# A scheduled SSM convolution and feed-forward kernel: GpSimd's powers planned around VectorE's port, idle matmuls on zeros ahead of the taps, and a full-height skip row

## The chip, the cores and the metric

The kernel runs on one core of a Trainium2 chip. The time is the device time of that core in microseconds (us), the median of several executions. A ratio is the mean time of one kernel's runs over the mean time of the other kernel's runs of the same rounds, on the same chip; it is therefore not quite the ratio of the medians that are quoted beside it. The brackets after a ratio are its 95% interval. A profile shows a single execution, and single executions of one kernel differ here by about 1 us, at times more. So a profile is used to find where the time lies. Eviction means the copy of a result out of PSUM, the memory that PE writes to; X0 is the dense transform of the first block of VectorE's products.

## The reference, cut to what matters

```python
# q, k, v: 1 x 2048 x 640;  shift_k: 640 x 4;  ssm_k: 640 x 2048;  ssm_D: 640
k_shift = sum(k_pad[:, t:t+S, :] * shift_k[:, 3-t] for t in range(4))   # four taps
kv = k_shift * v
y  = irfft(rfft(kv_pad) * rfft(ssm_k_pad))[:S] + kv * ssm_D             # long convolution, skip row
a  = q * y
# ... residual and layer norm (two layers), then the feed-forward part:
out = (silu(h @ w_gate) * (h @ w_up)) @ w_down                          # 640 x 1728
```

The convolution is done as dense transforms on TensorE (PE) with products of spectra on VectorE (DVE). The rows are handled in four blocks.

## The kernel before

The program does not list its instructions in the order in which they run. It makes a list of operations with costs, and a small list scheduler, with priorities from a long table, gives each engine its order. Four parts matter here.

The load of k in two column halves on ScalarE's queue, and the warm-up matmuls:

```python
for c in range(2):
    dma([kin(0, 128, 3, 7, c)], 328, [], [(KIN0, f"m{c}")], -2001 + 2 * c, name="kin0", w=1.4, eng="act")
...
def warm(n):      # n = 8, placed after the taps and the transposes of k
    pt = PT("warm", "pC", 1)
    fns = [mm(lambda: B32(pt, 0, 512), lambda: V(IDN, 0, 128), lambda: V(TAPS, 0, 512), True, True) for _ in range(n)]
    pe(fns, 512, n, [(IDN, 0), (TAPS, (0, 0)), (TAPS, (0, 1))], tc(pt), -2000, name="warm")
```

The dense transform of k, with the skip row `D` added by a matmul whose operands have one row:

```python
def dense_h(nm, src, cells, h, dst, prio):
    for ri in range(2):
        fns = [mm(B32(pt, 0, CW), den(oFW(h, ri, b)), src(b), b == 0, b == R - 1) for b in range(R)]
        if nm[0] == "K" and ri == 0:
            fns[-1:] = [mm(B32(pt, 0, CW), V(ONE, 0, 128, 0, 1), V(DROW, int(nm[1]) * CW, CW, 0, 1), False, False)] + fns[-1:]
```

The layer norm, with its power on GpSimd (POOL) between two small VectorE instructions:

```python
vec(0.16, lambda v: v.tensor_scalar(out=va, in0=src, scalar1=k1, scalar2=LN_EPS, ...), ..., name="va")
P.op({"pool": 1.2}, lambda g: g.tensor_tensor(out=y, in0=va, in1=stt[:, 420:...], op=ALU.pow), ..., name="nr")
vec(0.16, lambda v: v.tensor_tensor(out=nm, in0=ng, in1=y, op=ALU.mult), ..., name="nm")
```

## Time and profile before

| | before |
|---|---|
| time | 299.29 us, 4 runs (299.08 to 300.37) |
| busy shares | PE 95%, VectorE 79%, ScalarE 68%, GpSimd 12% |
| first long product on VectorE | 9.31 us |
| first useful dense matmul | 12.40 us |
| start of the feed-forward matmuls (512 columns) | 60.99 us |
| last matmul starts | 294.36 us |
| VectorE idle for a power, up to 195 us | 0.93 + 0.92 + 0.59 + 0.93 us |

### The profile page before, as it was taken

To read this page: it belongs to the slowest core of one execution; us is meant where nothing else is said; L and a number is where in the kernel's file an instruction comes from. 1 tells how busy PE (TensorE), PEld (TensorE's weight loads), DVE (VectorE), ACT (ScalarE), POOL (GpSimd) and SP (SyncE) were. 2 spreads that over 40 slices of the span, in tenths; PEclk is the share of its full clock that TensorE was granted. 3 is DMA by queue.
4 is the path that set the end of the run, shared out by engine and by line. 5 is a ranking of instruction groups with operands and counts; after the bars stand their busy time and mean duration, and the time that the engine had idled before them with its cause. 6 is when DMAs were issued, how large, how long until landed. Compare 5 with 4: busy or idle time off the path is not lost.

```text
span 297.6 us, 5193 instructions
## 1 busy us (share of the span) xinstructions
PE 281.2 (95%) x1820; PEld 152.3 (51%) x1820; DVE 235.3 (79%) x475; ACT 201.3 (68%) x484; POOL 36.9 (12%) x32
## 2 busy tenths in 40 slices
PE   2999987899999999999999899989999999999996
PEld 1466653454544466654445366535444576444574
DVE  2799899989699999999999899986699852304422
ACT  3389899979997877988999794727989231351000
POOL 2000500341110205102001402200020020000000
PEclk9999999999999999999999999999999999999999
DMA  8999998657727693938621204766101034000002
GB/s 232 354 374 351 381 328 265 205 144 164 202 89 196 144 243 113 243 112 194 180 97 38 60 32 132 135 177 215 52 12 55 24 60 120 0 0 0 2 0 88
DMA packets 44051, 43.25 MB, mean 145 GB/s; under 512 B 14895, under 2 KB 38889, under 8 KB 43898
## 3 DMA queue, kind: packets, MB, share of 16 engines
q1 hardware_dynamic: 39640, 38.30, 41.3%
q0 software_dynamic: 3328, 3.97, 8.2%
q10 hardware_dynamic: 1058, 0.66, 0.8%
q8 instruction: 14, 0.23, 0.3%
q14 instruction: 11, 0.09, 0.1%
HBM read 20.63 MB, written 2.62 MB: 78 GB/s over the span
## 4 chain that ended last, share of the span: by engine, by line
PE 58%; DVE 21%; issue 9%; DMA 5%; POOL 4%; ACT 1%; ACTq 1%; POOLq 0%
PE ps L682 58%; DVE sb L900 16%; POOL stt L1006 4%; DMA sb<-sb 3%; DMA sb<-in_A_k_dram 2%; DVE stt L990 2%; ACT sb L665 1%; DVE sb L666 1%; DVE sb L1015 1%; ACTq L673 1%; DVE stt L994 0%; POOL sb L1076 0%; DVE sb L669 0%; DVE stt L1005 0%; DVE stt L1008 0%
## 5 line engine op out<-in xcount | busy, mean ns | idle before, releaser
L682 PE MATMUL ps<-sb 128*128 128x320 bf16 (+2 forms) x1220 | 226.8, 338 | 9.6 <-DMA sb<-in_A_shift_k_dram 5.3
L900 DVE TENSOR_TENSOR sb<-sb 128x1280 bf16<-128x1280 bf16 (+3 forms) x286 | 172.1, 660 | 6.2 <-ACT sb L665 2.8
L682 PEld LDWEIGHTS ps<-sb 128*128 128x128 bf16 (+2 forms) x1220 | 115.7, 98 | 103.1 <-issue 11.4
L665 ACT ACTIVATE sb<-ps 128x320 bf16<-128x320 f32 (+2 forms) x281 | 110.7, 477 | 28.2 <-PE ps L682 24.8
L682 PE MATMUL ps<-sb,tab 128*64 128x320 bf16 (+2 forms) x512 | 64.2, 302 | 3.1 <-DVE sb L900 1.5
L900 DVE TENSOR_TENSOR sb<-ps,sb 128x512 bf16<-128x512 f32 (+2 forms) x46 | 28.2, 617 | 42.8 <-PE ps L682 32.9
L1236 ACT ACTIVATE sb<-ps 128x512 bf16<-128x512 f32 (+1 forms) x56 | 33.6, 603 | 30.3 <-PE ps L682 29.8
L682 PEld LDWEIGHTS ps<-sb,tab 128*64 128x64 f16 (+2 forms) x512 | 31.5, 101 | 35.5 <-issue 9.0
L1006 POOL TENSOR_TENSOR stt<-stt 128x2 f32<-128x2 f32 (+1 forms) x12 | 22.7, 1895 | 143.1 <-DVE stt L1005 136.0
L1016 ACT ACTIVATE sb<-sb,stt 128x320 bf16<-128x320 bf16 (+1 forms) x35 | 24.4, 729 | 7.8 <-DVE stt L1008 6.9
L1076 POOL DMA_DIRECT2D sb<-sb x12 | 12.4, 1035 | 60.7 <-DVE sb L900 34.0
L668 ACT ACTIVATE sb<-ps 128x320 bf16<-128x320 f32 x46 | 17.7, 438 | 0.7 <-PE ps L682 0.4
L666 DVE CAST sb<-ps 128x320 bf16<-128x320 f32 x27 | 12.8, 483 | 5.7 <-PE ps L682 5.6
L990 DVE BATCH_NORM_STATS2 stt<-sb 128x6 f32<-128x320 bf16 x32 | 14.4, 478 | 0.0
L1036 ACT ACTIVATE sb<-sb,stt 128x640 bf16<-128x640 bf16 x16 | 13.3, 832 | 0.0
L1029 ACT ACTIVATE sb<-sb 128x640 bf16<-128x640 bf16 x16 | 12.0, 750 | 0.0
L1015 DVE TENSOR_SCALAR sb<-sb,stt 128x320 bf16<-128x320 bf16 (+1 forms) x13 | 5.1, 395 | 0.0
L669 DVE TENSOR_SCALAR sb<-ps 128x320 bf16<-128x320 f32 x10 | 4.7, 486 | 0.2 <-PE ps L682 0.2
L1008 DVE TENSOR_TENSOR stt<-stt 128x2 f32<-128x2 f32 (+1 forms) x12 | 1.8, 148 | 3.4 <-POOL stt L1006 3.4
L810 PE MATMUL ps<-sb 128*128 128x128 bf16 (+1 forms) x48 | 3.9, 231 | 0.3 <-ACT sb L668 0.3
L810 PEld LDWEIGHTS ps<-sb 128*128 128x128 bf16 (+1 forms) x48 | 3.2, 120 | 1.7 <-issue 1.4
L1210 PE MATMUL ps<-sb 128*128 128x128 bf16 x40 | 3.4, 220 | 0.4 <-ACT sb L665 0.4
(21 smaller groups left out, 23.6 us busy)
## 6 DMA issues: line engine op xcount, KB each, us to landing
sb<-sb SPq DMA_DIRECT2D x72, 160.0 KB, 2.3
sb<-sb POOLq DMA_DIRECT2D x12, 320.0 KB, 4.5
out_dram<-sb SPq DMA_DIRECT2D x16, 160.0 KB, 1.8
sb<-in_A_k_dram SPq DMA_DIRECT2D x8, 280.0 KB, 4.2
sb<-in_B_w_down_dram SPq DMA_DIRECT2D x13, 160.0 KB, 7.3
sb<-cst_den SPq DMA_DIRECT2D x8, 256.0 KB, 6.7
sb<-in_A_q_dram SPq DMA_DIRECT2D x6, 320.0 KB, 3.7
sb<-in_A_v_dram SPq DMA_DIRECT2D x6, 320.0 KB, 3.4
```

The costliest lines, as they stand in the source:

```text
L665: fns = {"act": lambda a: a.activation(out=dst(), in_=src(), func=ACTF.Copy), "dve": lambda v: v.tensor_copy(out=dst(), in_=src())}
L666: "dve": lambda v: v.tensor_copy(out=dst(), in_=src())}
L668: fns = {"act": lambda a: a.activation(out=dst(), in_=src(), func=ACTF.Copy, scale=scale), "dve": lambda v: v.tensor_scalar(out=dst(), in0 ...
L682: return lambda t: t.matmul(o(), l(), r(), start=st, stop=sp)
L900: return lambda v: v.tensor_tensor(out=o(), in0=a(), in1=b_(), op=op)
L990: vec(dve1(CW, False), lambda v: v.bn_stats(st6(l, j, b, c), V(xt, b * D + c * CW, CW)), [(xt, (b, c))], [(ST, ("s", l, j, b, c))], prio, ...
L1006: P.op({"pool": 1.2}, lambda g: g.tensor_tensor(out=y, in0=va, in1=stt[:, 420:420 + hi - lo], op=ALU.pow), c1 + [(ST, "half")], c3, prio, ...
L1016: "act": lambda a: a.activation(out=dst(), in_=src(), func=ACTF.Identity, scale=rs(l, j, b), bias=tmv(l, j, 3)[:, b:b + 1])},
L1029: P.op({"act": act_c(D) + 0.22}, lambda a, b=b, jt=jt: a.activation(out=V(jt, 0, D), in_=V(xt, b * D, D), func=ACTF.Copy, accum_out=tmv(l, ...
L1036: P.op({"act": act_c(D) + 0.3}, lambda a, b=b, jt=jt: a.activation(out=V(jt, 0, D), in_=V(xt, b * D, D), func=ACTF.Square, bias=tmv(l, j, ...
L1076: P.op({"pool": 1.35}, [lambda g: g.dma_start(v4(t0), src(), accum_op=ALU.add)], [(t0, 0)] + cells, [(t0, 0)], prio, dma=(2.1, 2.1, 0.8), ...
L1236: P.op({"act": act_c(n)}, lambda a: a.activation(out=dst(), in_=src(), func=ACTF.Silu), rd, wr, -1000, name=f"si{nm}", after=after)
```

## The change

Its intent: the scheduler learns that a GpSimd power and a two-input VectorE instruction shut each other out, and plans the powers where VectorE does something else. The warm-up of PE moves into time in which PE is idle anyway. The skip row loses its drain by using all 128 rows, of which 127 are zeros. All priorities of the table are new.

```diff
+        o.lock = "dve" in engs and (name[:2] in ("m1", "m2", "ac", "kv", "cr", "ci", "hn", "nm") or ...)
...
+                    waits = e == "dve" and free["pool"] <= t + 1e-9 and any(<a power has been ready for 0.6 us>)
+                        if e == "pool" and o.dma is None and c > 0.5 and free["dve"] > t + 1e-9 and dvelock:
+                            continue
+                        if e == "dve" and o.lock and (poolend > t + 1e-9 or waits):
+                            continue
...
-        P.op({"pool": 0.1}, lambda g: g.memset(V(ONE, 0, 128, 0, 1), 1.0), [], [(ONE, 0)], ...)
+        vec(0.2, lambda v: v.memset(V(ONE, 0, 128), 0.0), ...)
+        vec(0.2, lambda v: v.memset(V(ONE, 0, 128, 0, 1), 1.0), ...)
...
-            warm(8)
+        vec(0.4, lambda v: v.memset(V(WD, 12 * D, D), 0.0), ...)
+        for _ in range(4):
+            pt = PT("warm", "pC", 1)
+            pe([mm(B32(pt, 0, 512), V(WD, 12 * D, 128), V(WD, 12 * D, 512), True, True) for _ in range(2)], 512, 2, ..., -2990, name="warm")
...
-  mm(B32(pt, 0, CW), V(ONE, 0, 128, 0, 1), V(DROW, int(nm[1]) * CW, CW, 0, 1), False, False)
+  mm(B32(pt, 0, CW), V(ONE, 0, 128),       V(DROW, int(nm[1]) * CW, CW),       False, False)
...
-            P.op({"pool": 1.2}, lambda g: g.tensor_tensor(out=y, ..., op=ALU.pow), ...)
+            P.op({"pool": 0.75}, lambda g: g.tensor_tensor(out=y, ..., op=ALU.pow), ...)
```

The lock rule lives in the scheduler alone. It adds no semaphore: on the chip nothing holds VectorE back where the plan has a hold.

## The prediction

> **What bounds the kernel now.** I read the page's shares first, then the 40 slices, then the start engine by engine, then every wait of PE, and last GpSimd.
>
> ```profile
> PE 281.2 (95%) x1820; PEld 152.3 (51%) x1820; DVE 235.3 (79%) x475; ACT 201.3 (68%) x484; POOL 36.9 (12%) x32
> ...
> PE   2999987899999999999999899989999999999996
> PEld 1466653454544466654445366535444576444574
> DVE  2799899989699999999999899986699852304422
> ```
>
> One slice is 7.44 us. VectorE is at 8 or 9 tenths nearly everywhere from slice 2 to slice 25 (about 192 us), and PE is at 9 almost throughout, so the two bound the kernel together up to about 195 us; after that PE alone does, with matmuls back to back. No new arithmetic can save much: the gain must come from PE time that does no useful work. I add it up. The first matmul starts at 5.27 us, the last at 294.4, and 3 us of eviction and store follow. Within that the single matmul starts show 10.7 us of gaps longer than 0.25 us above the streaming pitch: 6.4 us of them between 22.8 and 57 us, 0.35 at 67.2, 0.54 at 117.1, 0.61 and 1.06 at 164.5 and 166.2, 1.77 at 192.9. To these come the warm-up matmuls and the skip rows, below.
>
> The start, as PE and its weight loads saw it:
>
> ```profile
> 8.36 2.12 PE L682 MATMUL ps<-sb 1*128 1x320 bf16 x5
> 9.42 6.77 PE L682 MATMUL ps<-sb 128*128 128x512 bf16 x29
> ...
> 11.12 0.15 PEld L682 LDWEIGHTS ps<-sb 128*128 128x128 bf16 x1 [0.28 <-issue]
> 11.55 0.15 PEld L682 LDWEIGHTS ps<-sb 128*128 128x128 bf16 x1 [0.27 <-issue]
> 11.98 0.15 PEld L682 LDWEIGHTS ps<-sb 128*128 128x128 f16 x1 [0.28 <-issue]
> 12.40 0.35 PEld L682 LDWEIGHTS ps<-sb 128*128 128x128 f16 x2 [0.28 <-issue]
> 13.02 0.62 PEld L682 LDWEIGHTS ps<-sb 1*128 1x128 bf16 x5 [0.26 <-issue]
> 13.90 1.71 PEld L682 LDWEIGHTS ps<-sb 1*128 1x128 bf16 x13 [0.26 <-issue]
> ```
>
> Groups are merged by operand, so starts matter more than counts. Loads at 11.12, 11.55, 11.98 are 0.427 us apart for 512 columns: half the later speed. These are the eight warm-up matmuls, 9.02 to 12.40, 3.4 us. The first useful dense matmul starts only at 12.40, and from 12.65 the pitch of 320 columns is 0.136 us. At 13.02 and 13.90 a load of one row (the skip row) sits behind a 0.26 us hole. VectorE in the same stretch, with the end of the chain of waits that leads to it:
>
> ```profile
> 2.40 6.88 DMA sb<-in_A_k_dram
> ...
> 9.31 1.56 DVE L900 TENSOR_TENSOR sb<-sb 128x1280 bf16<-128x1280 bf16 x2 [2.22 <-DMA sb<-in_A_k_dram]
> 10.79 0.48 DVE L666 COPY sb<-ps 128x640 bf16<-128x640 bf16 x1
> 11.19 11.66 DVE L900 TENSOR_TENSOR sb<-sb 128x1280 bf16<-128x1280 bf16 x17
> ```
>
> VectorE begins its long run at 9.31, when the ACT queue's second k load lands (issued 2.40), and is then never free. The first block of eight products ends at 16.3, and PE's first X0 matmul starts at 16.36: from there VectorE leads and PE follows. GpSimd's powers:
>
> ```profile
> 162.21 0.16 DVE L1005 TENSOR_SCALAR stt<-stt 128x4 f32<-128x4 f32 x1
> 162.28 3.02 DVE L900 TENSOR_TENSOR sb<-sb 128x1280 bf16<-128x1280 bf16 x5
> 166.23 0.16 DVE L1008 TENSOR_TENSOR stt<-stt 128x4 f32<-128x4 f32 x1 [0.93 <-POOL stt L1006]
> ...
> 162.45 3.75 POOL L1006 TENSOR_TENSOR stt<-stt 128x4 f32<-128x4 f32 x1 [21.66 <-DVE stt L1005]
> ...
> 240.71 0.89 POOL L1006 TENSOR_TENSOR stt<-stt 128x2 f32<-128x2 f32 x1 [2.03 <-DVE stt L1045]
> ```
>
> The same power on a handful of numbers takes 0.89 us once and 3.75 us another time. At 162 VectorE runs five tensor_tensors with no gap until 165.30, and the power ends 0.90 us after that. It had not been slow, it had not begun. Four of the twelve are like this (3.89, 3.40, 3.95, 3.75 us), and VectorE then stands idle for 0.93, 0.93, 0.59 and 0.93 us: 3.4 us in all.
>
> **What the Trainium skill says.** "SBUF — State Buffer", section "Who interferes with whom": a DVE instruction with two SBUF inputs contends with a GpSimd instruction that reads SBUF, and the lock holds for a whole instruction. The trace agrees (3.75 against 0.89 us); it also shows that a power can be kept out by a whole back-to-back row. "TensorE: Matmul & The Clock Gate", Part 1: the array clock is at half until one free-running window of about 3.4 us has been busy. Agrees: 0.427 us per 512 columns up to 12.4 us, 0.216 later; the clock record turns at 12.63, although PE had been active since 5.27. The same page, "LDWEIGHTS": the time depends on columns, not rows, so a full-height skip row should cost no more than a one-row one. "TensorEngine Tiling (Array Packing)", "Key Properties": changing the tiling mode drains the array. The trace agrees for a one-row matmul between full ones: pitch 0.232 before it, 0.237 on it, 0.146 after, against 0.136.
>
> **The change part by part.** PE has 1820 matmuls in both kernels, and VectorE's and ScalarE's instruction lists are the same but for three or four evictions and norms that swap engines. So it moves work and removes none.
>
> *Skip row.* 0.232 + 0.237 + 0.146 - 3 x 0.136 = 0.207 us saved each, eight of them: 1.65 us of PE. It costs three VectorE memsets of about 0.33 us or less before 4 us, when VectorE is idle. Six of the eight lie after 13.9 us, all in the stretch where VectorE leads, so I count about half, 0.8 us.
>
> *Warm-up.* Two groups of four zero matmuls now run on PE from about 1.7 us (two memsets of 0.33 after VectorE's first instruction at 0.99), with two tap matmuls between them. 8 x 0.427 = 3.4 us leave the stretch 9.0 to 12.4. The dense matmuls can start once the k transposes are evicted (about 8.6 us as now) and their tables are there: the first table landed at 10.4 us in the trace and is now queued three transfers (about 900 KB; at some 300 GB/s 3 us) earlier, so 7.5. But X0 waits for VectorE's eight products anyway: the dense start moves by 3.8 us, PE's pace does not. PE will have finished the K0 dense work before X0 is ready and will stand idle a little.
>
> *VectorE's start*, which the diff does not tell and the order of instructions does. Before, the ACT queue issued the wrong k half first (0.74, landed 5.0), taps, then the half that the first product needs (2.40, landed 9.29). Now it issues taps, the activation table load, then the needed half. I put its issue at 3.0 us (0.74 + 0.95 + 1.28) and its landing at 3.0 + 4.3 (what the first load took) = 7.3: VectorE starts 2.0 us earlier. Five evictions instead of two come before the products' end (3 x 0.48 = 1.4 us), so X0 is only 0.6 us earlier, but those evictions are missing later: in summed durations, VectorE's work up to the power of the first second-layer norm is the same to 0.5 us. So 2.0 us lead.
>
> *Powers.* I read what stands on VectorE between each power's input and its use. Second-layer powers are now followed by statistics, aggregates or PSUM copies, and the 3.95 us one by a single product: the 0.59 us goes. The first-layer powers still have 6, 7 and 15 products and PSUM products after them, though some of these wait for PE or ScalarE and leave a hole. I expect half of their 3 x 0.93 us to go. Of PE's gaps, those at 117.1, 164.5 and 166.2 (2.2 us) hang on such powers. Together 1.8 us in PE's end, not the 11 us by which the four powers are too long: work for PE and VectorE lay beside most of that.
>
> *New order.* All priorities are new. The 1.77 us wait at 192.9 for a shuffle can go or another can come; I give it 0.7 us.
>
> Sum: 2.0 + 0.8 + 1.8 + 0.7 = 5.3 us; 299.45 - 5.3 = 294.1.
>
> **The rivals.** First, PE's waste is the whole story, and the new order turns most of it into time: 3.4 + 1.65 + most of the 10.7 us would give some 10 us, 289 to 290. For it: PE ends the kernel with about 95 us of unbroken matmuls, so what PE gains before 195 us counts in full. Against it: VectorE is 97% busy from 9.3 to 190 us and its work is unchanged. Second, a transfer takes the place: the early stage moves 350 to 380 GB/s with DMA at 9 tenths, the table of tap weights or the second k half comes later, VectorE starts at 9.3 as before, and only powers and skip rows count: 296.5 to 297.5. Third, the powers stay locked out because nothing in the machine holds VectorE back where the plan assumes a hold; VectorE runs its row and the plan drifts: 0 to 2 us lost on the sum, 294 to 296.
>
> **Range and chances.** The mean of these, with the first at a quarter, the second at a fifth, gives 294; the first sets the low end, the second the high one: 290.5 to 297.6. Two per cent is 293.5, close to my middle, so faster by over 2% has 0.42, within 2% 0.56. Slower would need a new long wait; 0.02.
>
> **What would show it.** VectorE's first long product at about 7.3 us instead of 9.31; the first dense matmul near 8.6 and at a pitch of 0.136, and X0 at 15 to 16; no 0.26 us holes before skip rows; the clock at full before 8.6. No second-layer power over 1.6 us; one or two first-layer ones still near 3. PE gaps over 0.25 us of 7 to 8 us in place of 10.7. The prediction is wrong if VectorE's products begin at 9 us or later, if the zero matmuls leave the clock at half when the dense ones start, or if new PE waits for shuffles appear after 100 us.

## More of the kernel before

The prediction shows the shares, the start and the powers. Two more lines of the page of before show what the end hangs on: the first gives the shares of the chain of waits that ended last by engine, the second the group of VectorE's products (busy us, mean ns of one, then the idle time just before them).

```profile
PE 58%; DVE 21%; issue 9%; DMA 5%; POOL 4%; ACT 1%; ACTq 1%; POOLq 0%
...
L900 DVE TENSOR_TENSOR sb<-sb 128x1280 bf16<-128x1280 bf16 (+3 forms) x286 | 172.1, 660 | 6.2 <-ACT sb L665 2.8
```

GpSimd has 4% of the chain, about 12 us, although its powers hold handfuls of numbers. That is what the change aims at.

## The result, and the profile after

| | before | after |
|---|---|---|
| time, first comparison (4 runs each) | 299.29 us (299.08 to 300.37) | 297.08 us (296.94 to 297.44), ratio 0.9921 [0.9895, 0.9947] |
| time, second comparison, another chip | 300.94 us, 11 runs (299.57 to 301.57) | 297.10 us, 6 runs (296.25 to 298.18), ratio 0.9883 [0.9859, 0.9906] |
| first product / second product on VectorE | 9.31 / 10.05 us | 7.49 / 10.03 us |
| first useful dense matmul | 12.40 us | 10.38 us |
| matmul pitch turns to full clock | 12.6 us | 15.3 us |
| start of the feed-forward matmuls | 60.99 us | 60.86 us |
| from there to the last matmul | 233.37 us | 231.27 us |
| VectorE idle for a power, up to 195 us | 3.37 us in four | 1.84 us in two |

The change is 2.2 us faster where 5.3 us were predicted. In the second comparison it is 3.5 to 3.8 us; a likely reason for the difference is given below. The page of after, shares, slices and the chain by engine:

```profile
PE 282.1 (96%) x1820; PEld 153.8 (52%) x1820; DVE 235.6 (80%) x479; ACT 200.1 (68%) x484; POOL 33.2 (11%) x31
...
PE   7898978799999899999999999999999999999996
...
DVE  3999899998999899999999999992899743214422
...
PE 71%; DVE 15%; ACT 4%; DMA 4%; POOL 3%; issue 2%; SPq 1%; ACTq 0%; DVEq 0%
```

PE is at 7 in the first slice, where it was at 2: that is for the most part the idle work on zeros, and no gain. From slice 15 on PE shows 9 without a break, and the chain hangs on it for 71% and no longer 58%. GpSimd's share fell from 4% to 3% only.

VectorE's timeline at the start of after (start, duration, engine, line, operation, operands, count, and the idle time before it with what ended it):

```profile
7.08 0.49 DVE L678 CAST sb<-ps 128x320 bf16<-128x320 f32 x1 [3.39 <-PE ps L694]
7.49 0.81 DVE L913 TENSOR_TENSOR sb<-sb 128x1280 bf16<-128x1280 bf16 x1
8.22 0.88 DVE L678 CAST sb<-ps 128x320 bf16<-128x320 f32 x2
9.62 0.49 DVE L678 COPY sb<-ps 128x640 bf16<-128x640 bf16 x1 [0.51 <-PE ps L823]
10.03 1.67 DVE L913 TENSOR_TENSOR sb<-sb 128x1280 bf16<-128x1280 bf16 x2
```

The first product begins 1.8 us earlier, as predicted. But in VectorE's queue two tap casts and the copy of the transposed k stand before the second one, and the copy waits 0.51 us for PE. The Trainium skill, "PSUM — Partial Sum Buffer", section "Engine vs sequencer instructions", says that VectorE's queue is strictly first in, first out, and the trace agrees: the second product begins at 10.03, right behind the copy. In before it began at 10.05, with no copy in front of it. So the first block of eight products, after which PE's X0 can start, ends at 16.32, where it ended at 16.30; the prediction had X0 0.6 us earlier. PE's timeline of after shows why the copy is late:

```profile
1.71 1.89 PE L694 MATMUL ps<-sb 128*128 128x512 bf16 x4 [1.71 <-DVE sb L728]
3.84 4.33 PE L694 MATMUL ps<-sb 1*128 1x320 bf16 x12 [0.25 <-DVE sb L711]
8.23 1.35 PE L823 MATMUL ps<-sb 128*128 128x128 bf16 x12
10.38 11.13 PE L694 MATMUL ps<-sb 128*128 128x320 bf16 x63 [0.80 <-ACT sb L677]
```

The second group merges eight one-row tap matmuls with four idle ones of 512 columns. The idle ones stand between the taps, and the transposes of k (line 823) come at 8.23; in before they came at 7.05. The dense matmuls follow at 10.38, not at 8.6 as predicted, and the first 19 of them run at a pitch of 0.267 us, which is half speed. The single starts show the pitch of 0.136 only from 15.4 us. There is no hole of 0.26 us before a skip row any more.

The two long powers of after on GpSimd, and VectorE around them:

```profile
30.75 3.72 POOL L1019 TENSOR_TENSOR stt<-stt 128x4 f32<-128x4 f32 x1 [26.35 <-DVE stt L1018]
67.12 5.19 POOL L1019 TENSOR_TENSOR stt<-stt 128x4 f32<-128x4 f32 x1 [11.46 <-DVE stt L1018]
```

```profile
30.57 2.99 DVE L913 TENSOR_TENSOR sb<-sb 128x640 bf16<-128x640 bf16 x6
34.50 0.16 DVE L1021 TENSOR_TENSOR stt<-stt 128x4 f32<-128x4 f32 x1 [0.94 <-POOL stt L1019]
66.95 4.50 DVE L913 TENSOR_TENSOR sb<-sb 128x512 bf16<-128x512 bf16 x7
72.35 0.16 DVE L1021 TENSOR_TENSOR stt<-stt 128x4 f32<-128x4 f32 x1 [0.90 <-POOL stt L1019]
```

The power of 5.19 us is longer than any of before. VectorE runs seven two-input products from 66.95 to 71.45, and the power ends 0.86 us after the last of them: the lock-out is as before, in these two places of the plan. The third first-layer power took 2.28 us at 162.95, the longest second-layer one 1.20, and both end while VectorE has other work; so the waits of 0.59 and 0.93 us at 117 and 166 us are gone. (The power at 237 us has a new wait of 0.59 us behind it, in the stretch where VectorE has time.)

**Where the 2.2 us came from.** The kernel is cut at the first feed-forward matmul. The first part gained 60.99 - 60.86 = 0.13 us, the second 233.37 - 231.27 = 2.10 us. In the second part the single matmul starts show these waits of more than 0.25 us above the pitch: before, 0.35 at 67.2, 0.54 at 117.1, 0.61 and 1.06 at 164.5 and 166.2, 1.77 at 192.9, in all 4.33; after, 0.69 at 81.3 and 1.30 at 102.1, in all 1.99. The difference is 2.34, which is all of the gain. The waits of 0.35, 0.54 and 1.06 us, 1.95 us in all, hung on powers: they are gone in the kernel before without powers (an experiment below). The one of 0.61 us is not: it ends when ScalarE's eviction comes, and the same kernel without powers has it too, with 0.63 us. PE's timelines, first of before, then of before without powers (the bracket counts from the modelled end of the matmul and is shorter):

```profile
165.31 1.25 PE L682 MATMUL ps<-sb 128*128 128x512 bf16 x5 [0.45 <-ACT sb L665]
```

```profile
165.07 1.25 PE L682 MATMUL ps<-sb 128*128 128x512 bf16 x5 [0.47 <-ACT sb L665]
```

The rest is 2.38 us before, 1.77 of it behind a shuffle (a transfer from SBUF to SBUF), and 1.99 us after, all behind shuffles.

### The profile page after: what moved, and what is told of

Same layout as the page of the kernel before. It is cut to its first block, busy times and chain, and to the rows that moved or that the text cites. A ratio compares the mean times of both kernels' runs of the same rounds, so it can differ in the third digit from the quotient of the medians.

```text
span 295.3 us, 5206 instructions
## 1 busy us (share of the span) xinstructions
PE 282.1 (96%) x1820; PEld 153.8 (52%) x1820; DVE 235.6 (80%) x479; ACT 200.1 (68%) x484; POOL 33.2 (11%) x31
## 4 chain that ended last, share of the span: by engine, by line
PE 71%; DVE 15%; ACT 4%; DMA 4%; POOL 3%; issue 2%; SPq 1%; ACTq 0%; DVEq 0%
PE ps L694 70%; DVE sb L913 12%; DMA sb<-sb 4%; POOL stt L1019 3%; ACT sb L677 3%; ACT sb L1029 1%; DVE stt L1003 1%; DVE sb L678 1%; ACT sb L680 1%; SPq L685 1%; PE ps L823 0%; DVE sb L1028 0%; PE ps L1223 0%; DVE sb L779 0%; DVE sb L681 0%
## 5 line engine op out<-in xcount | busy, mean ns | idle before, releaser
L694 PE MATMUL ps<-sb 128*128 128x320 bf16 (+1 forms) x1220 | 227.7, 341 | 6.1 <-DVE sb L913 1.9
L694 PEld LDWEIGHTS ps<-sb 128*128 128x128 bf16 (+1 forms) x1220 | 116.9, 99 | 99.9 <-issue 7.7
L694 PE MATMUL ps<-sb,tab 128*64 128x320 bf16 (+2 forms) x512 | 63.1, 302 | 3.0 <-DMA sb<-sb 1.7
L1019 POOL TENSOR_TENSOR stt<-stt 128x2 f32<-128x2 f32 (+1 forms) x12 | 19.2, 1603 | 134.6 <-DVE stt L1018 94.8
L1029 ACT ACTIVATE sb<-sb,stt 128x320 bf16<-128x320 bf16 (+1 forms) x31 | 22.3, 751 | 7.0 <-DVE stt L1021 6.6
L680 ACT ACTIVATE sb<-ps 128x320 bf16<-128x320 f32 x49 | 18.5, 447 | 5.1 <-PE ps L694 4.9
L678 DVE CAST sb<-ps 128x320 bf16<-128x320 f32 x26 | 12.0, 481 | 3.4 <-PE ps L694 3.4
L1028 DVE TENSOR_SCALAR sb<-sb,stt 128x320 bf16<-128x320 bf16 (+1 forms) x17 | 6.2, 384 | 0.7 <-DMA sb<-sb 0.7
L823 PEld LDWEIGHTS ps<-sb 128*128 128x128 bf16 (+1 forms) x48 | 3.2, 120 | 1.9 <-issue 1.6
L681 DVE TENSOR_SCALAR sb<-ps 128x320 bf16<-128x320 f32 x7 | 3.3, 481 | 0.4 <-PE ps L694 0.4
```

The costliest lines, as they stand in the source:

```text
L678: "dve": lambda v: v.tensor_copy(out=dst(), in_=src())}
L680: fns = {"act": lambda a: a.activation(out=dst(), in_=src(), func=ACTF.Copy, scale=scale), "dve": lambda v: v.tensor_scalar(out=dst(), in0 ...
L694: return lambda t: t.matmul(o(), l(), r(), start=st, stop=sp)
L1019: P.op({"pool": 0.75}, lambda g: g.tensor_tensor(out=y, in0=va, in1=stt[:, 420:420 + hi - lo], op=ALU.pow), c1 + [(ST, "half")], c3, prio, ...
L1029: "act": lambda a: a.activation(out=dst(), in_=src(), func=ACTF.Identity, scale=rs(l, j, b), bias=tmv(l, j, 3)[:, b:b + 1])},
```

## The experiments

Each kernel was compared with the kernel before in the same rounds. The first was the changed kernel again; its result stands in the table above (297.10 us, ratio 0.9883). Its first part ended at 60.85 us, within 0.01 us of the first run of it.

> The changed kernel again, as the yardstick for the runs beside it: 297.1 us, 0.992 of before. Nothing is told apart by it; it narrows the interval.

**One row again.** The skip row of the changed kernel back to one row, all else kept.

```diff
- V(ONE, 0, 128), V(DROW, int(nm[1]) * CW, CW)
+ V(ONE, 0, 128, 0, 1), V(DROW, int(nm[1]) * CW, CW, 0, 1)
```

> The changed kernel with the skip row as a one-row matmul again, order of all instructions unchanged. Theory (VectorE sets the pace until about 60 us, and all eight skip rows lie before that): at most +0.4 us on the changed kernel, 297.1 to 297.5, and PE's gaps over 0.25 us before 60 us shrink by what the holes take (about 1.6 us). Rival (PE's own time sets the end everywhere): 8 x 0.207 = +1.65 us, about 298.7.

Measured: 297.33 us (297.03 to 298.26), 0.9889 [0.9867, 0.9911], beside 297.10 and 0.9883 for the changed kernel. By the prediction's count the eight skip rows take 1.65 us more of PE, and the time moves by 0.2 us, less than the interval. PE's gaps of over 0.25 us between 22.8 and 57 us, 7.3 us in the changed kernel, are 4.6 us in this one: what the full height saves on PE turns into waiting beside VectorE's work. (This profile is one of the two slowest runs, with the clock at half from 55.6 to 59.0 us.)

**Full height in the kernel before.** The reverse: only the skip row changed, in the old order.

```diff
- lambda g: g.memset(V(ONE, 0, 128, 0, 1), 1.0)
+ [lambda g: g.memset(V(DROW, 0, D), 0.0), lambda g: g.memset(V(ONE, 0, 128), 1.0)]
- V(ONE, 0, 128, 0, 1), V(DROW, int(nm[1]) * CW, CW, 0, 1)
+ V(ONE, 0, 128), V(DROW, int(nm[1]) * CW, CW)
```

> The kernel before with nothing changed but the skip row to full height (ones on all rows, the skip vector's other rows zeroed by GpSimd). Theory (VectorE sets the pace there): 0 to -0.4 us on 299.3. Rival (PE sets it): -1.65 us, about 297.6, which would be most of what the whole change gained.

Measured: 300.41 us (298.07 to 301.52), 0.9981 [0.9949, 1.0013]. That is 0.6 us at the most likely value and not told from nothing.

**Short idle matmuls.** The eight idle matmuls of 512 columns become four of 16 columns.

```diff
-  pe([mm(B32(pt, 0, 512), V(WD, 12 * D, 128), V(WD, 12 * D, 512), True, True) for _ in range(2)], 512, 2,
+  pe([mm(B32(pt, 0, 16), V(WD, 12 * D, 128), V(WD, 12 * D, 16), True, True)], 512, 2,
```

> The changed kernel with its eight idle matmuls cut from 512 to 16 columns and four groups of one, everything else in the same order. Theory (they never warmed the clock in the profiled run, and only held back taps and k transposes on PE, and through them VectorE's second product): taps done 1.5 us earlier, the first dense matmul near 8.8 instead of 10.38, VectorE's first block of eight ends near 15.3 instead of 16.33; -0.5 to -1.0 us. Rival (they warm the clock and are worth their place): clock full later than 15.3 us and +1 to +2 us.

Measured: 296.71 us (296.48 to 297.04), 0.9863 [0.9843, 0.9884]. The idle matmuls gain nothing and may cost 0.4 to 0.6 us (0.9883 - 0.9863 = 0.002 of 300.9; the intervals overlap). The dense matmuls start at 9.15 us, the second product at 8.84, and the pitch turns to full at 15.09 us all the same, beside 14.98 with the long ones. The first part of the kernel is 1.04 us shorter (59.81), the second 1.5 us longer than in the profile of the changed kernel of the same call (231.90 and 230.43).

**Long idle matmuls.** Two groups of eight idle matmuls of 512 columns without a break, the others one of 16 columns.

```diff
+  for nw in range(4): 512 columns and eight of them where nw is 1 or 2, else 16 columns and one
```

> The changed kernel with sixteen idle matmuls on zeros, eight before and eight behind the first tap, instead of four and four; a look at the clock, not a faster kernel. If zeros count as activity, 3.4 us of unbroken zeros before the first tap and another 3.4 behind it put the clock at full between 5.1 and 9 us, and the first dense matmul runs at 0.136 us. If they do not count, the clock turns only after 3.4 us of dense matmuls, later than 14 us, as in the four profiles so far (15.3, 15.0, 15.1, 13.5). Time: 1 to 3 us above the changed kernel, for taps and k transposes come later.

Measured: 301.46 us, one run, state unknown. This table of stretches of its profile gives busy us and count by engine, then the granted TensorE clock, the DMA share and GB/s:

```profile
7.50:10.80 3.30, 2.91 (x13) 0.87 (x11) 0.70 (x2) 1.34 (x4) 0.00 (x0) 1.00 1.02 371
10.90:17.60 6.70, 5.85 (x30) 3.42 (x29) 6.08 (x10) 2.04 (x5) 0.00 (x0) 0.50 1.10 330
```

The clock record turns to full at 7.46 us. (Before that it shows 1.00 too, but has no entry yet: the starts are 0.427 us apart, half speed.) From 10.87 to 17.70 it is at 0.50. So in this one run matmuls on zeros do count: the clock turned during the fourteenth of sixteen without a break. And what they bring is lost again in the stretch of one-row taps, transposes and short idle times that follows, before the dense matmuls begin at 13.39. A warm-up in this place did not last until the dense matmuls.

**The right half of k first.** In the kernel before, the two k loads on ScalarE's queue change places after scheduling; nothing else.

```diff
+        a = P.order["act"]
+        i, j = [n for n, o in enumerate(a) if o.name == "kin0"]
+        a[i], a[j] = a[j], a[i]
```

> The kernel before with one edit: the ACT queue issues the k half that the first product needs before the other half. Theory (VectorE's row from its first product to about 60 us sets the pace, so an earlier start of it is worth most of its length): first product at 7.1 instead of 9.3, end of the first block of eight near 14.1 instead of 16.3, and 1 to 2 us off the time. Rival (what is won at the start is given back at later fixed waits): the same first numbers, and under 0.5 us off the time.

Measured: 298.70 us (297.81 to 299.43) beside 300.82 (299.89 to 303.26), 0.9924 [0.9899, 0.9949]. Two swapped lines give 2.1 to 2.3 us, about two thirds of what the whole change gave in the second comparison (0.9883), on another chip. VectorE's timeline:

```profile
6.75 1.56 DVE L900 TENSOR_TENSOR sb<-sb 128x1280 bf16<-128x1280 bf16 x2
...
8.62 7.47 DVE L900 TENSOR_TENSOR sb<-sb 128x1280 bf16<-128x1280 bf16 x9
17.76 4.30 DVE L900 TENSOR_TENSOR sb<-sb 128x640 bf16<-128x640 bf16 x8 [1.66 <-ACT sb L665]
```

Here nothing stands between the first and the second product, and the head start is used until 16.1 us, where VectorE has to wait for PE's X0 and its eviction.

**Swap and full height together**, in the old order.

```diff
+  the edits of the two experiments above, on the kernel before
```

> The kernel before with two small edits and its old order: the needed k half first, and the full-height skip row. Theory (the start is worth 2.3 us by the earlier run, the skip row 0 to 0.6): 0.990 of before, and so as good as the whole change. Rival (the change's new order is what gained): 0.992 or higher, clearly behind the changed kernel's 0.988.

Measured: 298.00 us (297.35 to 298.41), 0.9908 [0.9877, 0.9939]. The full height adds at most little: 0.0016 more than the swap alone, on another chip. The two small edits reach 0.0092 of the changed kernel's 0.0117, and the intervals overlap: whether the new order gains anything beyond them is not settled.

**No powers in the kernel before.** The power becomes a multiplication by one on VectorE, right behind its input. Its output is wrong, which doesn't matter for the time.

```diff
-  P.op({"pool": 1.2}, lambda g: g.tensor_tensor(out=y, in0=va, in1=stt[...], op=ALU.pow), ...)
+  P.op({"pool": 1.2}, lambda v: v.tensor_scalar(out=y, in0=va, scalar1=1.0, scalar2=None, op0=ALU.mult), ...)
+  # after scheduling: each moved to VectorE's order, right behind its input
```

> The kernel before with GpSimd's twelve powers replaced by a small VectorE multiply (wrong numbers on purpose, 0.15 us each, right behind the power's input). It shows the most that any planning around the lock can give. Theory (prediction's term, 1.8 us, plus the gap it counted separately): -2 to -3 us on before, PE gaps at 164 to 167 and at 117 us gone. Rival (powers lie beside other work): under 1 us.

Measured: 299.12 us (298.22 to 300.48), 0.9943 [0.9915, 0.9970], so 1.7 us faster. The twelve multiplications are not free: start to start, one lengthens VectorE's row by about 0.2 us (in the same edit of the changed kernel, the instruction after the input starts 0.27 us behind it and no longer 0.07). Up to 195 us there are nine, so up to 1.8 us. By these figures the powers of before cost 1.7 to 3.5 us. In the trace PE's waits at 67.2, 117.1 and 166.2 us are gone, as expected for the last two; the one at 164.5, which was expected to go, stays, and PE's wait for the shuffle behind them is 2.26 us and no longer 1.77.

**No powers in the changed kernel.** The same edit; the result is wrong here too.

> The same replacement in the changed kernel. Theory (the change left the first-layer powers locked out: 3.72 and 5.19 us, with VectorE idle 0.94 and 0.90 us behind them): another -1 to -2 us on the changed kernel. Rival (the change took out all that powers cost): within 0.5 us of it.

Measured: 296.80 us (296.60 to 300.57), 0.9893 [0.9852, 0.9934], as the changed kernel itself (0.9883). (Two of its six runs, 298.74 and 300.57, have a lower mean clock, 0.988 and 0.994; the other four lie within 296.60 to 296.83.) It does not follow that powers cost nothing any more: the multiplications' 1.8 us may balance the 0.94 + 0.90 us of waits that are left, and the trace shows a second candidate. The feed-forward matmuls start at 60.31 and no longer at 60.85 us, but PE then waits 1.85 us for a shuffle that lands at 102.20 us, beside 0.82 for it in the changed kernel's second profile. Both edits add the same multiplications. In the old order the edit brings 1.7 us, in the new one nothing, which argues that the change has taken away some 1.7 us of what the powers cost (2.0 with 0.9893 against 0.9883); the waits for shuffles, which moved in both, are in these figures.

**VectorE held back.** In the changed kernel the instruction that uses a first-layer power moves to right behind the power's input, so that VectorE waits and can't lock GpSimd out.

```diff
+        for o in [o for o in d if o.name[:3] == "nm0"]:
+            d.remove(o)
+            d.insert(<1 + position of the last of its inputs>, o)
```

> The changed kernel with VectorE's use of each first-layer power moved to right behind the power's input, so that VectorE stands still and the power can begin at once. Right numbers. Theory (a plan's hold does nothing on the chip unless an instruction waits): the four first-layer powers take 0.8 to 1.2 us each instead of 3.72, 5.19, 2.28, 1.52; VectorE idle is no longer than before; -0.5 to -1.5 us. Rival (that latency lies beside other work): same within 0.5 us.

Measured: 300.38 us (299.80 to 300.68), 0.9978 [0.9955, 1.0001]. My theory missed. GpSimd's and VectorE's timelines of this kernel at the power that had been the longest:

```profile
67.28 1.01 POOL L1019 TENSOR_TENSOR stt<-stt 128x4 f32<-128x4 f32 x1 [11.39 <-DVE stt L1018]
```

```profile
68.32 0.17 DVE L1021 TENSOR_TENSOR stt<-stt 128x4 f32<-128x4 f32 x1 [1.12 <-POOL stt L1019]
```

The power falls from 5.19 to 1.01 us, and the kernel gets slower: 0.9978 - 0.9883 is 0.0095 of 300.8, or 2.9 us, over two comparisons. VectorE now waits at all four first-layer powers (1.16, 1.12, 1.15, 1.12, in all 4.55 us) and no longer 1.84 us at two: 2.7 us more idle time became 2.9 us more time. A long power cost nothing here while VectorE worked; the idle time that the hold added came back in full. (It need not: of the 2.45 us behind the last three long powers of before, 1.95 reached PE as waits.) This also shows that the lock is what makes a power long: alone it takes about 1.0 us.

**Four early evictions to ScalarE**, once in the changed kernel and once with the short idle matmuls. This was to clear VectorE's queue between its first products.

```diff
+        for o in [o for o in d[:20] if o.name in ("tap1", "tap2", "tap3", "deK0h1")]:
+            d.remove(o)
+            a.insert(<by planned start>, o)       # d: VectorE's order, a: ScalarE's
```

> The changed kernel, idle matmuls kept, with the same four evictions moved to ScalarE. Theory as above: -1.0 to -1.6 us on the changed kernel (0.988), so 0.983 to 0.985. Rival: the second product still waits for the late taps and k transposes, X0 where it was, and 0.987 to 0.988.

Measured: 296.93 us (296.27 to 297.54), 0.9874 [0.9842, 0.9905].

> The changed kernel without idle matmuls and with four early evictions (taps 1 to 3, one K0) moved from VectorE to ScalarE, which is half idle there. Theory (VectorE is busy without a gap from its first product to 57 us, so each 0.4 us taken off it is won): 4 x 0.40 = 1.6 us earlier by 20 us, -1.0 to -1.6 us against the run without idle matmuls (0.986), so 0.981 to 0.983. Rival (PE's cold dense matmuls bind once VectorE is faster): X0 starts no earlier than 15.3, and 0.985 to 0.987.

Measured: 297.16 us (296.43 to 298.00), 0.9887 [0.9851, 0.9922]. Neither is told from its parent (0.9883 and 0.9863); the rival was right. The copy of the transposed k stayed on VectorE, so the second product still came at 10.11 and 8.89 us. With the casts gone VectorE stood idle in front of that copy instead, for 0.88 us in the first of the two kernels:

```profile
9.70 0.49 DVE L678 COPY sb<-ps 128x640 bf16<-128x640 bf16 x1 [0.88 <-PE ps L823]
```

So it is the copy, and PE's transposes before it, that hold the second product, and not the casts.

**Where the second part's waits come from.** In the profiles of before, after and the kernel with short idle matmuls PE's longest wait in the second part is for a shuffle. The chain of waits of the kernel with short idle matmuls, around its longest:

```profile
98.13 4.08 DMA sb<-sb
...
102.45 5.57 PE ps L694 x37
```

The trace's records of landings show more: the parts of this shuffle land from 100.10 us on, the last one at 102.21. A single 16 KB packet of the queue that the profile calls "instruction" starts at 99.41 us and takes 1.47 us. In the kernel before, nine shuffles that SyncE issued between 60 and 200 us have parts that land over 1 us apart, and in eight of them such a packet falls between issue and landing; so it does for the 1.77 us wait at 192.9 us (packet at 192.69). Four kernels were to move these packets without changing any work, by adding instructions to PE's stream: 15 tiny idle matmuls in PE's idle time, or the idle or warm-up matmuls cut into smaller ones.

```diff
   # on the short idle matmuls: the group that runs first gets 16 matmuls of 16 columns
+  ... for _ in range(16 if _ == 2 else 1)]
   # on the kernel before: 32 of 128 columns (split), 16 of 256 (split2); on the changed kernel: 32 of 128
-  B32(pt, 0, 512) ... V(TAPS, 0, 512) ... for _ in range(n)
+  B32(pt, 0, 128) ... V(TAPS, 0, 128) ... for _ in range(4 * n)
```

> The variant with four tiny idle matmuls in place of eight long ones (296.7 us), with 15 more tiny ones of 16 columns while PE is idle before the taps: 30 more instructions in PE's stream, nothing else changed. Theory (fetches of PE's instructions hold up one part of a shuffle): the 16 KB packets come about 2.2 to 2.6 us earlier (99.4 to about 97, 77.4 to about 75), the shuffle issued near 98.1 lands all its parts within 0.6 us, PE's wait at about 100.5 falls from 1.9 us to below 0.7, and the time falls by 0.5 to 1.2 us, to 295.5 to 296.2. Rival (VectorE and PE are in step there anyway): the wait stays at over 1.3 us and the time at 296.4 to 297.0.

Measured: 296.12 us (295.68 to 296.63) beside 300.16 (299.61 to 300.85), 0.9865 [0.9848, 0.9882]. The packet moved from 99.41 to 97.29, as expected, the one before it did not (77.45 to 78.10). The shuffle at 98 us no longer held PE; the one issued at 93.69, with the packet now in it, did:

```profile
97.77 1.03 PE L694 MATMUL ps<-sb 128*128 128x512 bf16 x4 [0.16 <-ACT sb L677]
99.69 1.25 PE L694 MATMUL ps<-sb,tab 128*64 128x320 bf16 x9 [0.90 <-DMA sb<-sb]
```

The time lies in the range that the theory gave, but the kernel before ran faster too, and the ratio is that of its parent. The wait changed its place and part of its length, and the time stayed.

> The kernel before with its eight warm-up matmuls of 512 columns cut into 32 of 128 columns: the same columns, 24 matmuls and 48 instructions more in PE's stream. Theory: the packets come about 3 to 4 us earlier from there on (192.7 to about 189), the shuffles issued at 190 to 192 land within 1 us of their first part, PE's wait of 1.77 us at 192.9 falls below 0.5, and the time falls by 0.8 to 1.8 us. Rival: the warm-up takes the same 3.4 us, nothing else moves, and the time is within 0.4 us of before.

Measured: 300.07 us (298.86 to 300.49), 0.9987 [0.9968, 1.0005]. The packet came at 190.74 and no longer at 192.69, the wait at 193 to 195 us was 0.81 and no longer 1.77, and the time moved by 0.4 us at the most likely value. The rival was right on the time.

> The kernel before with its warm-up cut into 16 matmuls of 256 columns: a third of the dose of the 32, 16 instructions more. Theory: the packets come about 1.0 to 1.3 us earlier (192.7 to about 191.5), so the one there ends at about 192.4, still in the way of the shuffle issued first but before the others: the wait at 192.9 falls to about half (0.5 to 1.3 us) and the time by 0.3 to 1.2 us. Rival: within 0.4 us of before.

Measured: 300.32 us (299.45 to 302.00), 1.0011 [0.9986, 1.0037]. The packet came at 195.02 in a profile that ran later as a whole, and the wait was 1.89 us. Nothing moved.

> The changed kernel with its eight idle matmuls of 512 columns cut into 32 of 128 columns. Theory: the packets come 3 to 4 us earlier (101.1 to about 97.5, 79.8 to about 76), PE's waits at 81.3 (0.69) and 102.1 (1.30) fall to less than half, and the time falls by 0.4 to 1.5 us to 295.6 to 296.7. Rival: within 0.3 us of the changed kernel's 297.1.

Measured: 297.97 us (297.19 to 300.46), 0.9942 [0.9910, 0.9974]: if anything slower than the changed kernel. The packet that I meant to move came at 101.68, where it had been at 101.06. The profile of this kernel is its slowest run, with the clock at half from 81.20 to 84.62 us, so its waits are not read. The theory that these packets are a cost that can be moved away at will has fallen. That late parts of shuffles and these packets come together is seen in the traces; that the one causes the other was not isolated.

## Why the prediction was wrong, point by point

The time of 297.08 us lies inside the range of 290.5 to 297.6, near its edge, and "within 2%" had the larger chance. The change was mis-sized: 5.3 us predicted, 2.2 us measured in that comparison.

**VectorE's start: the step that failed.** The prediction put the needed half of k at 7.3 us (measured: 7.49) and counted "so 2.0 us lead". It had seen five evictions where there had been two, and argued that "those evictions are missing later". The runs show that the feed-forward start goes with the second product and not with the first. Times in us; "feed-forward" is the start of the first matmul of 512 columns behind the dense stage:

| kernel | first product | second product | feed-forward | feed-forward minus second product |
|---|---|---|---|---|
| before | 9.31 | 10.05 | 60.99 | 50.94 |
| before, no powers | 10.14 | 10.88 | 61.77 | 50.89 |
| before, full height | 10.35 | 11.09 | 62.24 | 51.15 |
| after | 7.49 | 10.03 | 60.86 | 50.84 |
| after, second comparison | 7.96 | 10.02 | 60.85 | 50.83 |
| after, VectorE held back | 7.84 | 10.02 | 61.24 | 51.22 |
| short idle matmuls | 6.90 | 8.84 | 59.81 | 50.97 |
| short idle matmuls, padded | 7.50 | 9.44 | 60.32 | 50.87 |
| before, right half first | 6.75 | 7.49 | 59.82 | 52.33 |

In the first eight rows the last column is nearly constant, 50.8 to 51.2, while the first product moves by 3.5 us: the feed-forward start follows the second product. (The last kernel has its 1.66 us wait at 16.1 us on top; the same holds for the swap with full height, 52.55, with a wait of 1.30. With one skip row the difference is 51.88, with VectorE idle for 0.91 us at 19.5 us and the clock at half from 55.6 to 59.0 us in that run. Left out of the table are the changed kernel without powers, 50.30; the two with evictions moved, 51.39 and 51.38; long idle matmuls, 51.75; and the three with cut-up idle or warm-up matmuls, 51.15, 51.82 and 51.70. So the rule holds to about 1 us.) In the changed kernel 10.03 - 7.49 = 2.54 us pass between the two products, in before 0.74. So the term of 2.0 us measured 0.1 us. The work moved ahead did not come back as a lead, because the copy among it, which has to wait for PE's transposes, was put before the very products that the path waits for.

The table also suggests why the change gains more in the second comparison. The start of before hangs on a load, which lets the first product begin at 9.31 us in its one profile, but at 10.14 to 11.01 us in four kernels that share its start and ran on other chips; their feed-forward starts are 61.8 to 63.3. One of them, the full height in the kernel before, ran on the chip of the second comparison, beside the changed kernel at 60.85: there the first part is worth about 62.24 - 60.85 = 1.4 us.

**Skip row: 0.8 us predicted, none seen.** The holes went, as predicted, and 1.65 us of PE time with them. Taking them back in costs 0.2 us, less than the interval. The prediction counted half of the gain because two of the eight lie before VectorE leads; but the first part follows VectorE's second product, and PE's saving never reaches the end.

**Warm-up: no gain predicted, right; its clock claim was wrong.** Pace did not follow the dense start. But "the clock at full before 8.6" failed: full at 15.3 us, later than before (12.6). (The turn varies with the same start: 13.50 to 18.01 us in six profiles of the new order with its idle matmuls, 12.60 to 14.58 in five of the old order with its warm-up, so how much later is not settled.) Eight idle matmuls with taps between them did not wake the clock, sixteen with no break did (7.46 us, one run), and in the one-row work after them it was lost again. The dense start came at 10.38 and not at 8.6: the idle matmuls themselves had pushed the transposes back by 1.2 us. They are the part of the change that can be taken out without loss.

**Powers: 1.8 us predicted, about 1.7 measured, and by the way that was told.** The 0.59 us at 117 went, the 0.93 us at 166 went, those at 33 and 71 us stayed (0.94 and 0.90): 1.53 us less idle time on VectorE up to 195 us. PE lost waits of 1.95 us that hung on powers. The prediction's 2.2 us counted the 0.61 at 164.5, which does not hang on a power, and left out the 0.35 at 67.2, which does. The pair of kernels without powers says 1.7. "One or two first-layer ones still near 3" was right in kind (3.72 and 5.19). (The prediction set 3.75 us beside 0.89 as the same power; the 0.89 is one on 128x2 numbers, and one on 128x4 takes 1.01 when VectorE is held back.) The third rival, powers that stay locked out because nothing in the machine holds VectorE, is true for these two; the experiment that did hold VectorE shows that a hold would have been worse.

**New order: 0.7 us predicted, 0.4 measured.** The waits of 0.61 us at 164.5 and, for a shuffle, of 1.77 at 192.9 went, and two others for shuffles came (0.69 and 1.30 us). PE's gaps over 0.25 us, in the prediction's own count from 22.8 us on, came to 9.3 us and not to 7 to 8: those up to 57 us grew from 6.4 to 7.3. The prediction named "new PE waits for shuffles after 100 us" as a sign that it is wrong; the one at 102 us came.

**The sum, as measured in the first comparison:** start and skip row 0.13, powers 1.95 of PE's waits, the other waits 0.39, together 2.5 against 2.23 us by which the last matmul starts earlier (294.36 to 292.13). Of the 3.1 us by which the prediction is too high, about 2.7 are the start and the skip row, which the path did not feel.

**What stays open.** The lock rule and the new priorities were not separated: no run has the one without the other. Kernels of the new order that start earlier give part of it back in the second part: 231.90 us with short idle matmuls and 231.34 padded, against 230.43 and 231.27 in the two profiles of the changed kernel. They meet the others at the shuffles of 97 to 102 us. Whether the late parts of those shuffles, VectorE's pace or both set that point was not settled by the four last kernels.

**A better version.** The changed kernel with short idle matmuls has the lowest ratios, 0.9863 and, padded, 0.9865 on another chip, beside 0.9883 for the changed kernel. The intervals overlap, so the gain of some 0.5 us over the changed kernel is possible and not proven. Over the kernel before it is clear, at about 1.4%.

## What to carry to other kernels

Follow a head start through the in-order queue of the engine that leads: what counts is when the work that the path needs gets through, not when the first instruction of it starts. Before a new plan is credited, try the smallest edit of the old one: here swapping two loads gave two thirds of the gain. A long instruction on a side engine is worth shortening only if the engine that sets the pace stands idle for it; giving it way by a hold cost more here than the wait.

## What the Trainium skill lacked or had wrong

- "TensorE: Matmul & The Clock Gate", Part 1, gives the half clock and a busy window of about 3.4 us, but not what counts as busy. Here matmuls on zeros count (full at 7.46 us, after about 5.8 us of them without a break from 1.71 us; one run), while eight of them mixed with one-row taps and transposes did not (full at 15.3 us, with PE active from 1.71 us). In the run with sixteen the full clock was lost 3.4 us later (10.87 us) although PE was busy for 2.91 us of 3.30 before. The page has the loss come after an idle window, or after short frequent idles to which it gives no size. Here four profiles lost the full clock for 3.41 us in mid-kernel, after 3.41 us in which PE was busy, by the modelled ends, for 2.19 us (one row again, lost at 55.55), 2.34 (the changed kernel with evictions moved, 54.85), 2.19 (long idle matmuls, 58.66) and 1.43 (idle matmuls cut up, 81.20).
- "SBUF — State Buffer", section "Who interferes with whom", tells of a lock that one instruction holds. It does not say that a row of two-input VectorE instructions without a gap keeps a GpSimd instruction out for the whole row: 5.19 us for a power on 128x4 numbers that takes 1.01 us when VectorE is held back.
- "Runtime: NRT & Kernel Launch", "Instruction fetch mechanics", does not say what the 16 KB blocks in which instructions are fetched do to a kernel's own transfers. Here the "instruction" queue has some 14 packets of 16 KB in a run, 0.9 to 1.7 us each. In the kernel before, eight shuffles with such a packet between issue and landing landed their last part 1.4 to 2.6 us after the first; six others with one took 0.3 to 1.0. The connection is one in time; it was not isolated.
- "TensorEngine Tiling (Array Packing)", "Key Properties", says that a change of the tiling mode drains the array and gives no duration. Here a one-row matmul between full ones made the three starts around it 0.207 us longer in all than full-height ones.
